# A gated recurrence with a highway layer: pairs of tokens, turned as 32-bit elements

## The chip, the cores and the metric

The kernel runs on one core of one Trainium2 chip. The metric is the device time of one execution in microseconds (us). Before the change three runs took 226.25, 229.24 and 226.26 us, a median of 226.26 us.

A core has five engines that matter here, each with its own instruction queue that it works through in order: TensorE (PE in the profile; its weight loads are listed apart, as PEld), VectorE (DVE), ScalarE (ACT), GpSimd (POOL), and SyncE (SP), which only issues transfers. Transfers between the chip's memory (HBM) and the on-chip memory (SBUF) run on 16 DMA engines. TensorE writes its results to a small memory of its own, PSUM, which VectorE and ScalarE can read.

## The reference, cut to what matters

```python
# x, f_logit: 4 sequences x 6336 tokens x 256 channels, float32
sig = 1.0 / (1.0 + np.exp(-f_logit))
f = lower_bound + (1.0 - lower_bound) * sig      # decay, per token and channel
i = 1.0 - f
for t in range(S):
    h = f[:, t] * h + i[:, t] * x[:, t]          # a scan along the tokens of each sequence
    y[:, t] = h

# then, over all 25344 tokens, with y in the place of x:
H = np.maximum(y @ w_h, 0.0)
T = 1.0 / (1.0 + np.exp(-(y @ w_t + b_t)))
out = T * H + (1.0 - T) * y
```

## The kernel before, in words

The 25,344 tokens are cut into units. Most units are 1024 consecutive tokens of one sequence; the two first units hold 192 tokens of each of two sequences, the first sequence's first 1024 tokens are cut into two units of 512, and the last 1024 into units of 512, 256 and 256. Units of different sequences alternate.

Tokens come from HBM with the tokens on the partitions: a tile `lt` (gate logits) and a tile `xt` (inputs) of 128 partitions x 8 token columns x 256 channels, float32. `load` (line 80) puts token `j*128 + p` of the unit into column `j` of partition `p`, so each piece that a transfer reads in HBM is one token's row, 256 x 4 bytes = 1 KB. The two first units use two transfers for each tile (line 84).

Per unit, these steps follow, each in a function of its own:

- `gate` (ACT, line 143): u = sigmoid(-f_logit) as 16-bit floats. Since i = (1 - lower_bound) * u, u is all that is needed of the gate.
- `product` (POOL, line 156): bv = u * x as bf16, in four instructions of two token columns each.
- `decay_pe` and `b_pe` (PE, lines 182 and 196): the recurrence runs along the tokens, and a scan runs along a partition. So u and bv are transposed on TensorE, 128 tokens x 128 channels at a time, into the PSUM tiles `uT` and `bT` with channels on the partitions and the unit's tokens in order along them. A transpose is a weight load of the 128 x 128 block followed by a matmul with an identity matrix. There are two channel halves (index `h` or `m`), so a full unit has 2 x 8 transposes of u and as many of bv.
- `decay_act` (ACT, line 189): f = 1 - (1 - lower_bound) * uT, for one channel half, out of PSUM.
- `scan` (DVE, line 207): h = f*h + bT, for one channel half, one instruction over the unit's tokens, bT read straight out of PSUM. The state here is y divided by (1 - lower_bound); the constant is put into the weights instead.
- `z_pe` and `g_pe` (PE, line 218): the two products with w_t and w_h, tiles `zp` and `gp`.
- `t_act` (ACT, line 231), `d_dve` and `e_dve` (DVE, lines 237 and 249, a quarter of e on POOL, line 251): the sigmoid, the maximum with the skip term subtracted, and their product.
- `o_pe` (PE, lines 267 and 268): y and e are turned back to tokens on partitions and summed in PSUM. `o_act` (ACT, line 276) copies them out and `store` writes them.

The main loop is a software pipeline written out by hand. In iteration n it issues the loads of unit n+4, the gate and product of n+2, the turning and decay of n+1, the scans of n, the two weight products and d, e of n-1, and the output of n-2. `pin` keeps the instructions of an engine in the order in which they are written, so each engine's queue is fixed. Every PSUM tile has one buffer: `bT` of one channel half can be written only when the scan of the half before has read it. `follow` makes the unit's first `product` instruction wait for the e of the same iteration on DVE.

On DVE an iteration is: scan of half 0, d of half 0, scan of half 1, d of half 1, e. On PE, `b_pe(n, 1)` stands between the two scans and before `z_pe(p, 1)`, and `b_pe(n + 1, 0)` is followed by `decay_pe(n + 1, 1)` and `g_pe(n, 0)`.

On SP the loads and stores stand in one queue. Loads run ahead of their use as far as five buffers for each of `lt` and `xt` allow. The transfers of all queues share eight completion counters, so that the ninth transfer waits for the first.

Of the kernel before, what the change touches and what calls it, by code (L numbers as in the profile page):

```python
# [11 lines left out]
FP32 = mybir.dt.float32  # L12
BF16 = mybir.dt.bfloat16
FP16 = mybir.dt.float16
AF = mybir.ActivationFunctionType
# [4 lines left out]
def kernel(  # L20
# [16 lines left out]
    nc = tc.nc  # L37
    B, S, D = x.shape
    assert D == 256
    P = 128  # L40
    NH = D // P
    NB = 8
# [5 lines left out]
    units = []  # L48
# [4 lines left out]
    for s0 in range(rest, S, NB * P):  # L53
        for b in range(B):
            last = s0 + NB * P == S and b == B - 1
            a = s0
# [5 lines left out]
    singles = ctx.enter_context(tc.tile_pool(name="singles", bufs=1))  # L62
    inp = ctx.enter_context(tc.tile_pool(name="inp", bufs=5))
    upool = ctx.enter_context(tc.tile_pool(name="upool", bufs=3))
    mid = ctx.enter_context(tc.tile_pool(name="mid", bufs=2))
# [5 lines left out]
    st = [dict() for _ in range(NU)]  # L71

    def pin(ins):
        return tc.keep_in_program_order(ins)

    def load(n, name, src):
        np_, nb, _, b, a = units[n]
        t = inp.tile([P, NB, D], FP32, tag=name, name=name)
        if isinstance(b, int):
            pin(nc.sync.dma_start(t[:, :nb], src[b, a:a + nb * P, :].rearrange("(j p) d -> p j d", p=P)))  # L80
        else:
            t4 = t[:np_, :nb].rearrange("p (b j) d -> p b j d", j=2)
            for j in range(2):
                pin(nc.sync.dma_start(t4[:, :, j], src[b, a + j * np_:a + (j + 1) * np_, :].rearrange("b p d -> p b d")))
        st[n][name] = t

    def store(n, j0, j1):
# [19 lines left out]
    for n in range(2):  # L107
        load(n, "lt", f_logit)
        load(n, "xt", x)

    ident_b = singles.tile([P, P], BF16, name="ident_b")
    make_identity(nc, ident_b)
    ident_h = singles.tile([P, P], FP16, name="ident_h")
    make_identity(nc, ident_h)

# [23 lines left out]

    def gate(n):  # L140
        np_, nb = units[n][:2]
        u = upool.tile([P, NB, D], FP16, tag="u")
        pin(nc.scalar.activation(u[:np_, :nb], st[n]["lt"][:np_, :nb], AF.Sigmoid, scale=-1.0))  # L143
        st[n]["u"] = u

    def follow(ins, after):

        if after is not None:
            tc.add_manual_dep(ins.ins, after.ins.name, mybir.DependencyInfo(
                mybir.DependencyClass.Sync, mybir.DependencyReason.DATA), reason="shared port")  # L150

    def product(n, after):
        np_, nb = units[n][:2]
        bv = mid.tile([P, NB, D], BF16, tag="bv")
        for q in range(0, nb, 2):
            ins = pin(nc.gpsimd.tensor_mul(bv[:np_, q:q + 2], st[n]["u"][:np_, q:q + 2], st[n]["xt"][:np_, q:q + 2]))  # L156
            if q == 0:
                follow(ins, after)
        st[n]["bv"] = bv

    def width(n):
        return units[n][0] * units[n][1]

    def both(n, m, key, make):


        if width(n) > 512:
            st[n][key, m] = make()
            yield st[n][key, m], m, 0
        elif m == 0:  # L170
            st[n][key, 0] = st[n][key, 1] = t = make()
            for k in range(NH):
                yield t, k, k * 512

    def col(n, m):
        return 0 if width(n) > 512 else m * 512

    def decay_pe(n, m):
        np_, nb = units[n][:2]
        for uT, h, c in both(n, m, "uT", lambda: ps1.tile([P, NB * P], FP16, tag="uT", name="uT")):  # L180
            for j in range(nb):
                pin(nc.tensor.transpose(uT[:, c + j * np_:c + (j + 1) * np_], st[n]["u"][:np_, j, h * P:(h + 1) * P],  # L182
                                        ident_h[:np_, :np_]))

    def decay_act(n, h):
        N, c = width(n), col(n, h)
# [3 lines left out]
                                 scale=ncc[:, h:h + 1], bias=1.0))  # L190

    def b_pe(n, m):
        np_, nb = units[n][:2]
        for bT, h, c in both(n, m, "bT", lambda: ps1.tile([P, NB * P], BF16, tag="bT", name="bT")):
            for j in range(nb):
                pin(nc.tensor.transpose(bT[:, c + j * np_:c + (j + 1) * np_], st[n]["bv"][:np_, j, h * P:(h + 1) * P],  # L196
                                        ident_b[:np_, :np_]))

    carry = {}

# [81 lines left out]
    for n in range(-3, NU + 2):  # L282
        if ok(n + 4) and n + 4 > 1:
            load(n + 4, "lt", f_logit)
            load(n + 4, "xt", x)
        p, pp = n - 1, n - 2
# [11 lines left out]
        if ok(n + 1):  # L298
            decay_pe(n + 1, 0)
            decay_act(n + 1, 0)  # L300
        if ok(p):
            d_dve(p, 0)
        if ok(n):
            b_pe(n, 1)
# [10 lines left out]
        if ok(n + 2):  # L315
            gate(n + 2)
# [5 lines left out]
        if ok(n + 1):  # L322
            b_pe(n + 1, 0)
            decay_pe(n + 1, 1)
            decay_act(n + 1, 1)
# [4 lines left out]
        if ok(n + 2):  # L330
            product(n + 2, after)
# [32 lines left out]
```

## Time and profile before

| | |
|---|---|
| runs | 226.25, 229.24, 226.26 us; median 226.26 |
| the profiled execution | 229.01 us; its span, from first to last instruction, 226.9 us |
| busy over the span | PE 195.0 us (86%), DVE 202.1 (89%), ACT 199.1 (88%), POOL 140.0 (62%) |
| data moved | 78.69 MB, 52.43 MB of it read; 60,262 packets, 53,584 of them under 2 KB |
| one 1024-token unit in the middle of the run | 7.92 us |

The page divides the span into 40 slices of 5.7 us and gives, for each, the busy share of each engine in tenths (9 is 90% or more), the clock that TensorE was granted in tenths, and the rate of the transfers. The table of groups gives for each line of the kernel and each engine the number of instructions, their busy time, the mean of one in ns, and the time that the engine sat idle before them with what ended it. A timeline lists instructions in order of time: start and duration in us, engine, line, output<-input, how many were merged. Matmuls overlap in the pipeline of TensorE and their ends are modelled, so the distance between starts says what one costs in a row of them, and the duration says when the result is there.

### The profile page before, as it was taken

Reading aid. Unit: us, or ns where it says so; the run is one execution under the profiler, and the core shown is the slowest. Engines: PE = TensorE matmul, PEld = TensorE weight load, DVE = VectorE, ACT = ScalarE, POOL = GpSimd, SP = SyncE. Lnnn points to the kernel's source line nnn. Section 1 sums busy time; section 2 is a strip of 40 time slices with the busy share of each in tenths; the row PEclk is TensorE's granted clock in tenths of the full one; section 3 lists DMA queues with packets and bytes.
Section 4 is the critical chain, followed back from the end, with each engine's and each line's share of the span. In section 5 each row is a group of like instructions: output and inputs, shape, how many; then the busy total and the mean of one; then the engine's idle time right before and its main releaser. Section 6 shows DMA issues by size and latency. Waiting matters only on the chain.

```text
span 226.9 us, 4999 instructions
## 1 busy us (share of the span) xinstructions
PE 195.0 (86%) x2008; PEld 136.9 (60%) x2008; DVE 202.1 (89%) x159; ACT 199.1 (88%) x198; POOL 140.0 (62%) x131
## 2 busy tenths in 40 slices
PE   0588495989999999999999999999999999998971
PEld 0356365656766666676666657666665766665661
DVE  1499657799999999999999999999999999999871
ACT  4459946799999999999999999999999999976873
POOL 2654870745966786696678669667866966764300
PEclk9999857899999999999999999999999999999998
DMA  6999999999999999999999999999999997542444
GB/s 179 307 386 386 383 390 390 390 390 387 399 385 385 399 394 389 384 397 382 382 391 395 388 390 402 395 384 403 396 387 397 396 349 276 202 185 95 185 185 185
DMA packets 60262, 78.69 MB, mean 347 GB/s; under 512 B 2384, under 2 KB 53584, under 8 KB 60240
## 3 DMA queue, kind: packets, MB, share of 16 engines
q1 hardware_dynamic: 59152, 77.86, 93.9%
q10 hardware_dynamic: 1088, 0.53, 0.9%
q8 instruction: 15, 0.25, 0.4%
q14 instruction: 7, 0.06, 0.1%
HBM read 52.43 MB, written 25.95 MB: 345 GB/s over the span
## 4 chain that ended last, share of the span: by engine, by line
DVE 52%; issue 23%; PE 13%; DMA 4%; ACT 3%; POOL 3%; DVEq 0%; SPq 0%; ACTq 0%; POOLq 0%
DVE y L207 25%; DVE d L237 19%; DVE e L249 8%; PE gp L218 4%; PE zp L218 3%; POOL bv L156 3%; DMA xt<-in_x_dram 2%; PE bT L196 2%; PE uT L182 2%; DMA lt<-in_f_logit_dram 1%; PE op L267 1%; PE op L268 1%; ACT o L276 1%; ACT u L143 1%; ACT t L231 1%
## 5 line engine op out<-in xcount | busy, mean ns | idle before, releaser
L156 POOL TENSOR_TENSOR bv<-u,xt 128x512 bf16<-128x512 f16 (+1 forms) x100 | 114.3, 1172 | 18.9 <-DMA xt<-in_x_dram 7.2
L207 DVE TENSOR_TENSOR_SCAN y<-f,y,bT 128x1024 bf16<-128x1024 f16 (+2 forms) x54 | 113.7, 2105 | 7.9 <-PE bT L196 7.6
L231 ACT ACTIVATE t<-zp,bt 128x1024 bf16<-128x1024 f32 (+3 forms) x58 | 56.9, 994 | 13.5 <-PE zp L218 13.5
L218 PEld LDWEIGHTS <-w_sb 128*128 128x128 f16 x408 | 39.7, 100 | 43.1 <-issue 10.0
L237 DVE SCALAR_TENSOR_TENSOR d<-y,ncc,gp 128x1024 bf16<-128x1024 bf16 (+3 forms) x58 | 63.8, 1101 | 1.0 <-PE gp L218 0.9
L189 ACT ACTIVATE f<-uT,ncc 128x1024 f16<-128x1024 f16 (+3 forms) x58 | 58.4, 1007 | 4.2 <-PE uT L182 4.2
L251 POOL TENSOR_TENSOR e<-d,t 128x512 bf16<-128x512 bf16 x22 | 25.5, 1159 | 56.3 <-PE gp L218 56.3
L218 PE MATMUL gp<-y,w_sb 128*128 128x512 bf16 (+2 forms) x204 | 53.3, 385 | 3.7 <-DVE d L237 1.3
L218 PE MATMUL zp<-y,w_sb 128*128 128x512 bf16 (+2 forms) x204 | 52.6, 382 | 0.1
L267 PE MATMUL op<-diag,y 128*128 128x128 f16 (+1 forms) x400 | 50.8, 221 | 2.2 <-ACT o L276 2.2
L276 ACT COPY o<-op 128x1024 f32<-128x1024 f32 (+2 forms) x51 | 50.9, 997 | 1.9 <-PE op L268 1.7
L143 ACT ACTIVATE u<-lt 128x2048 f16<-128x2048 f32 (+3 forms) x29 | 49.0, 1689 | 3.9 <-DMA lt<-in_f_logit_dram 3.9
L268 PE MATMUL op<-ident_b,e 128*128 128x128 bf16 (+1 forms) x400 | 50.8, 220 | 0.0
L268 PEld LDWEIGHTS <-e 128*128 128x128 bf16 (+1 forms) x400 | 44.9, 115 | 7.5 <-POOL bv L156 1.3
L267 PEld LDWEIGHTS <-y 128*128 128x128 bf16 (+1 forms) x400 | 45.0, 114 | 5.7 <-issue 0.3
L196 PE MATMUL bT<-ident_b,bv 128*128 128x128 bf16 (+1 forms) x400 | 32.8, 224 | 16.6 <-DVE y L207 8.3
L196 PEld LDWEIGHTS <-bv 128*128 128x128 bf16 (+1 forms) x400 | 26.9, 100 | 23.8 <-issue 15.2
L182 PE MATMUL uT<-ident_h,u 128*128 128x128 f16 (+1 forms) x400 | 32.4, 227 | 5.7 <-ACT u L143 5.7
L182 PEld LDWEIGHTS <-u 128*128 128x128 f16 (+1 forms) x400 | 26.1, 103 | 6.1 <-ACT u L143 5.7
L249 DVE TENSOR_TENSOR e<-d,t 128x1536 bf16<-128x1536 bf16 (+3 forms) x29 | 25.9, 892 | 3.6 <-ACT t L231 0.8
L207 DVE TENSOR_TENSOR_SCAN y<-f,bT 128x192 bf16<-128x192 f16 x8 | 3.9, 536 | 4.1 <-PE bT L196 4.1
L117 DVE TENSOR_SCALAR cc<-lb 128x2 f32<-128x2 f32 x1 | 0.2, 169 | 3.8 <-DMA lb<-in_lower_bound_dram 3.8
(16 smaller groups left out, 6.8 us busy)
## 6 DMA issues: line engine op xcount, KB each, us to landing
out_dram<-o SPq DMA_DIRECT2D x47, 512.0 KB, 7.2
lt<-in_f_logit_dram SPq DMA_DIRECT2D x22, 1024.0 KB, 9.4
xt<-in_x_dram SPq DMA_DIRECT2D x22, 1024.0 KB, 11.3
lt<-in_f_logit_dram SPq DMA_DIRECT2D x3, 512.0 KB, 7.6
xt<-in_x_dram SPq DMA_DIRECT2D x3, 512.0 KB, 6.7
lt<-in_f_logit_dram SPq DMA_DIRECT2D x4, 192.0 KB, 3.7
xt<-in_x_dram SPq DMA_DIRECT2D x4, 192.0 KB, 3.9
out_dram<-o SPq DMA_DIRECT2D x2, 384.0 KB, 9.3
```

Of the source, the lines that this page charges most:

```text
L143: pin(nc.scalar.activation(u[:np_, :nb], st[n]["lt"][:np_, :nb], AF.Sigmoid, scale=-1.0))
L156: ins = pin(nc.gpsimd.tensor_mul(bv[:np_, q:q + 2], st[n]["u"][:np_, q:q + 2], st[n]["xt"][:np_, q:q + 2]))
L182: pin(nc.tensor.transpose(uT[:, c + j * np_:c + (j + 1) * np_], st[n]["u"][:np_, j, h * P:(h + 1) * P], ident_h[:np_, :np_]))
L189: pin(nc.scalar.activation(st[n]["f"][:, h, :N], st[n]["uT", h][:, c:c + N], AF.Identity, scale=ncc[:, h:h + 1], bias=1.0))
L196: pin(nc.tensor.transpose(bT[:, c + j * np_:c + (j + 1) * np_], st[n]["bv"][:np_, j, h * P:(h + 1) * P], ident_b[:np_, :np_]))
L207: pin(nc.vector.tensor_tensor_scan(y[:, h, c0:c0 + ln], st[n]["f"][:, h, c0:c0 + ln], st[n]["bT", h][:, col(n, h) + c0:col(n, h) + c0 + ln ...
L218: pin(nc.tensor.matmul(p[:, c + a:c + e], w_sb[:, k, ki, h * P:(h + 1) * P], st[n]["y"][:, ki, a:e], start=ki == 0, stop=ki == NH - 1))
L231: pin(nc.scalar.activation(st[n]["t"][:, m, :N], st[n]["zp", m][:, c:c + N], AF.Sigmoid, bias=bt[:, m:m + 1]))
L237: pin(nc.vector.scalar_tensor_tensor(st[n]["d"][:, m, :N], st[n]["y"][:, m, :N], ncc[:, m:m + 1], st[n]["gp", m][:, c:c + N], op0=ALU.mult ...
L267: pin(nc.tensor.matmul(o, st[n]["y"][:, h, cols], diag[:, h], start=True, stop=False))
L268: pin(nc.tensor.matmul(o, st[n]["e"][:, h, cols], ident_b, start=False, stop=True))
L276: pin(nc.scalar.copy(st[n]["o"][:np_, j0:j1], st[n]["op"][:np_, :j1 - j0]))
```

## The change

Each partition now takes two neighbouring tokens, so that a load reads runs of two rows (2 KB): token `256k + 2p + j` goes to column `2k + j` of partition `p`. The two first units need one transfer for each tile instead of two.

The tiles `u` and `bv` keep the two 16-bit values of a channel side by side, in the order (token pair, channel, token of the pair). `gate` and `product` therefore write, and `product` reads, 16-bit elements with a step of two elements; their shapes and numbers stay.

The two 16-bit values together are taken as one float32 element for the transposes. `turn` transposes a 128 x 128 block of such elements, that is 256 tokens x 128 channels, against a float32 identity, into the same bytes of `uT` and `bT`: the 16-bit values land in token order, so decay, scan and all that follows read what they read before. A full unit has 2 x 4 such transposes of u and as many of bv. A third identity, `ident_f`, is made at the start.

```diff
+    def pairs(t):
+        return t.rearrange("p (k j) d -> p k (j d)", j=2)
+    def inner(t):
+        return t.rearrange("p k d j -> p k j d")
     def load(n, name, src):
...
-            pin(nc.sync.dma_start(t[:, :nb], src[b, a:a + nb * P, :].rearrange("(j p) d -> p j d", p=P)))
+            pin(nc.sync.dma_start(pairs(t[:, :nb]), src[b, a:a + nb * P, :].rearrange("(k p j) d -> p k (j d)", p=P, j=2)))
         else:
-            t4 = t[:np_, :nb].rearrange("p (b j) d -> p b j d", j=2)
-            for j in range(2):
-                pin(nc.sync.dma_start(t4[:, :, j], src[b, a + j * np_:a + (j + 1) * np_, :].rearrange("b p d -> p b d")))
+            pin(nc.sync.dma_start(pairs(t[:np_, :nb]), src[b, a:a + 2 * np_, :].rearrange("b (p j) d -> p b (j d)", j=2)))
...
+    ident_f = singles.tile([P, P], FP32, name="ident_f")
+    make_identity(nc, ident_f)
...
-        u = upool.tile([P, NB, D], FP16, tag="u")
-        pin(nc.scalar.activation(u[:np_, :nb], st[n]["lt"][:np_, :nb], AF.Sigmoid, scale=-1.0))
+        u = upool.tile([P, NB // 2, D, 2], FP16, tag="u")
+        pin(nc.scalar.activation(inner(u[:np_, :nb // 2]), st[n]["lt"][:np_, :nb].rearrange("p (k j) d -> p k j d", j=2),
+                                 AF.Sigmoid, scale=-1.0))
...
-        bv = mid.tile([P, NB, D], BF16, tag="bv")
-        for q in range(0, nb, 2):
-            ins = pin(nc.gpsimd.tensor_mul(bv[:np_, q:q + 2], st[n]["u"][:np_, q:q + 2], st[n]["xt"][:np_, q:q + 2]))
+        bv = mid.tile([P, NB // 2, D, 2], BF16, tag="bv")
+        for k in range(nb // 2):
+            ins = pin(nc.gpsimd.tensor_mul(inner(bv[:np_, k:k + 1])[:, 0], inner(st[n]["u"][:np_, k:k + 1])[:, 0],
+                                           st[n]["xt"][:np_, 2 * k:2 * k + 2]))
...
+    def turn(n, t, key, h, c):
+        np_, nb = units[n][:2]
+        for k in range(nb // 2):
+            pin(nc.tensor.transpose(t[:, c + 2 * k * np_:c + 2 * (k + 1) * np_].bitcast(FP32),
+                                    st[n][key][:np_, k, h * P:(h + 1) * P].rearrange("p d j -> p (d j)").bitcast(FP32),
+                                    ident_f[:np_, :np_]))
+
     def decay_pe(n, m):
...
-            for j in range(nb):
-                pin(nc.tensor.transpose(uT[:, c + j * np_:c + (j + 1) * np_], st[n]["u"][:np_, j, h * P:(h + 1) * P],
-                                        ident_h[:np_, :np_]))
+            turn(n, uT, "u", h, c)
...
     def b_pe(n, m):
...
-            for j in range(nb):
-                pin(nc.tensor.transpose(bT[:, c + j * np_:c + (j + 1) * np_], st[n]["bv"][:np_, j, h * P:(h + 1) * P],
-                                        ident_b[:np_, :np_]))
+            turn(n, bT, "bv", h, c)
```

In the built program each transpose is one weight load and one matmul, as before: 400 of each in the place of 800. On SP four transfers fall away, those of the two first units; on POOL two instructions come in at the start, for `ident_f`. The order of all engines is otherwise the same.

More of the change, by code (lines that the diff above doesn't have):

```diff
@@ L153, in product @@
         np_, nb = units[n][:2]
-        bv = mid.tile([P, NB, D], BF16, tag="bv")
-        for q in range(0, nb, 2):
-            ins = pin(nc.gpsimd.tensor_mul(bv[:np_, q:q + 2], st[n]["u"][:np_, q:q + 2], st[n]["xt"][:np_, q:q + 2]))
-            if q == 0:
+        bv = mid.tile([P, NB // 2, D, 2], BF16, tag="bv")
+        for k in range(nb // 2):
+            ins = pin(nc.gpsimd.tensor_mul(inner(bv[:np_, k:k + 1])[:, 0], inner(st[n]["u"][:np_, k:k + 1])[:, 0],
+                                           st[n]["xt"][:np_, 2 * k:2 * k + 2]))
+            if k == 0:
                 follow(ins, after)
@@ L176, in col @@
         return 0 if width(n) > 512 else m * 512
+    def turn(n, t, key, h, c):
[4 more added lines that the diff above has]
+                                    ident_f[:np_, :np_]))
     def decay_pe(n, m):
-        np_, nb = units[n][:2]
         for uT, h, c in both(n, m, "uT", lambda: ps1.tile([P, NB * P], FP16, tag="uT", name="uT")):
-            for j in range(nb):
-                pin(nc.tensor.transpose(uT[:, c + j * np_:c + (j + 1) * np_], st[n]["u"][:np_, j, h * P:(h + 1) * P],
-                                        ident_h[:np_, :np_]))
+            turn(n, uT, "u", h, c)
     def decay_act(n, h):
@@ L192, in b_pe @@
     def b_pe(n, m):
-        np_, nb = units[n][:2]
         for bT, h, c in both(n, m, "bT", lambda: ps1.tile([P, NB * P], BF16, tag="bT", name="bT")):
-            for j in range(nb):
-                pin(nc.tensor.transpose(bT[:, c + j * np_:c + (j + 1) * np_], st[n]["bv"][:np_, j, h * P:(h + 1) * P],
-                                        ident_b[:np_, :np_]))
+            turn(n, bT, "bv", h, c)
     carry = {}
```

## The prediction

> **What bounds the kernel now.** I read the slices of the page first, to see which engine is full and when.
>
> ```profile
> PE   0588495989999999999999999999999999998971
> DVE  1499657799999999999999999999999999999871
> ACT  4459946799999999999999999999999999976873
> PEclk9999857899999999999999999999999999999998
> GB/s 179 307 386 386 383 390 390 390 390 387 399 385 385 399 394 389 384 397 382 382 391 395 388 390 402 395 384 403 396 387 397 396 349 276 202 185 95 185 185 185
> ```
>
> After about 44 us three engines show 9 in every slice. The transfers stay at 385 to 400 GB/s and fall off from slice 32 (182 us), 40 us before the end: loads run ahead and are not awaited. The waits agree: ACT waited for `lt` three times (3.9 us) and POOL for `xt` three times (7.2 us), all before 14 us. So I asked for busy time in one period of the middle, 7.92 us (columns: PE, PEld, DVE, ACT, POOL, clock, DMA share, GB/s).
>
> ```profile
> 107.30:115.22 7.92, 7.50 (x81) 5.28 (x80) 7.82 (x6) 7.75 (x8) 5.67 (x6) 1.00 1.07 390
> ```
>
> DVE is busy for 7.82 us of 7.92, ACT for 7.75, POOL for 5.67. PE's 7.50 is modelled; distances of starts are safer. The timeline shows what stands between two scans:
>
> ```profile
> 105.56 0.61 PE L182 MATMUL uT<-ident_h,u 128*128 128x128 f16 x8
> 106.13 1.26 DVE L237 SCALAR_TENSOR_TENSOR d<-y,ncc,gp 128x1024 bf16<-128x1024 bf16 x1
> 106.26 0.61 PE L196 MATMUL bT<-ident_b,bv 128*128 128x128 bf16 x8
> 106.70 1.03 PE L218 MATMUL zp<-y,w_sb 128*128 128x512 bf16 x4
> 107.30 2.34 DVE L207 TENSOR_TENSOR_SCAN y<-f,y,bT 128x1024 bf16<-128x1024 f16 x1
> ```
>
> Eight transposes start over 0.44 us (106.26 to 106.70), 55 ns each, and their results are there at 106.87, 0.43 us before the scan at 107.30 can start behind d. Four matmuls of 512 columns start over 0.87 us (106.70 to 107.57). PE's demand per period is then 16 x 0.217 + 32 output matmuls x 0.055 + 32 transposes x 0.055 = 3.47 + 1.76 + 1.76 = 7.0 us of 7.92. DVE sets the period; PE has 0.9 us to spare, ACT 0.17, POOL 2.25.
>
> ```profile
> L156 POOL TENSOR_TENSOR bv<-u,xt 128x512 bf16<-128x512 f16 (+1 forms) x100 | 114.3, 1172 | 18.9 <-DMA xt<-in_x_dram 7.2
> L143 ACT ACTIVATE u<-lt 128x2048 f16<-128x2048 f32 (+3 forms) x29 | 49.0, 1689 | 3.9 <-DMA lt<-in_f_logit_dram 3.9
> L182 PE MATMUL uT<-ident_h,u 128*128 128x128 f16 (+1 forms) x400 | 32.4, 227 | 5.7 <-ACT u L143 5.7
> ```
>
> **What the Trainium skill says.** "TensorE: Matmul & The Clock Gate", Terms: weight loads and matmuls have a transpose mode that is "4× faster for FP32". No float32 transpose is in this trace, so nothing here confirms it. The same page, Weight-path perf modes: the fast weight load, on for 128 weights, is not used for FP32 input; LDWEIGHTS (loading the stationary operand) gives columns / 1.2 ns, 107 ns for 128. In the trace 16-bit loads last 98 ns but follow each other every 55 ns, so they overlap; float32 is not shown. "GPSIMD Engine Reference", Performance pitfalls: reads cost about half as much again once step x element size passes 8 bytes; here it becomes 4, and the trace has no stepped row. "SBUF — State Buffer", Door 1: up to 8 bf16 of step are free within a 16-byte line; the step here is two.
>
> **The change, part by part.** Call the cost of one float32 transpose in a row of them t.
>
> Transposes: removed are 32 x 0.055 = 1.76 us of PE per period, added 16 t. The low end of t is 55 ns, as for 16 bits (a gain of 0.88 us per period on PE, worth at most the 0.1 us of DVE idleness, 2 us in all); the high end is 4 x 55 = 222 ns, four passes. I take 110 ns, the skill's unhurried weight load with the matmul beside it: 16 x 0.110 = 1.76 us, nothing gained, nothing lost. Also, the first weight load of each group was done ahead of the wait for the scan (it ended at 106.05 for a matmul at 106.26); in the new program the wait stands before the weight load, so each of the groups behind a scan starts some 0.1 us later (estimate from the 98 ns). The cover is d: from the scan's end at 106.21, 0.06 + 0.10 + 4 x 0.110 + 0.17 to the last result gives 106.98, against 107.30. The other group, bT and uT in a row, must end before the d that frees `gp` at 102.89: 101.71 + 0.16 + 8 x 0.110 = 102.75. Both hold, so the period stays at 7.92 us. Without that cover each late 0.1 us would cost 20.6 x 0.1 = 2 us, since (207 - 44) / 7.92 = 20.6 periods run at DVE's pace. Behind the waiting transposes stand zp and gp, for which t (ACT) and d (DVE) wait.
>
> From which t does PE decide? 3.47 + 1.76 + 16 t + 0.2 (two late starts) = 7.92 at t = 156 ns.
>
> Gate: 22 full instructions of 1927 ns, same element count, output in steps of two. I take the same duration. Low end: nothing in the row could get shorter. High end, if each 16-bit write took twice its slot: +1.8 us per period, 1.6 us beyond ACT's spare time, +34 us. Product: four instructions at 1.14 us per period. I take the same; they could not be quicker than the equal-sized contiguous e on POOL (1159 ns); high end +50%: bv would end 2.3 us later. At 109.76 it ends now, and the scan that needs it starts at 111.79, about 0.3 us of transposing in between: 1.7 us of slack for the scan, less for PE behind it. Decides from about +25%.
>
> Loads: the same bytes in half as many packets. In the middle nobody waits for them, so a quicker transfer is worth nothing: the five buffers are the cover. At the start the rate is only 261 to 295 GB/s between 2 and 10 us, as the two `xt` transfers of unit 1 wait for counters of earlier ones; with four transfers fewer they need not, and `xt` of unit 1, which lands at 9.7 us on the chain that ended last, may come 2 us sooner. But w_sb, behind weights that land at about 10.8 us, is finished by DVE at 13.2 us, and the first gp starts at 12.8. So 2 us at most, 0 at least; I take 0.4. `ident_f` ends on POOL by some 2.4 us, while the first product waits until 5.90: free.
>
> Sum for the profiled execution: 229.0 + 0 - 0.4 = 228.6 us. It was 2.75 us above the median of the three runs, so against the median: 226.26 - 0.4, about 226.
>
> **The rivals.**
> *PE becomes the bound (slower).* At t = 222 ns PE needs 3.47 + 1.76 + 3.55 + 0.2 = 8.98 us per period, 1.06 more than DVE: 20.6 x 1.06 = 22, plus about 1 at the ends, 249 us. It decides from t = 156 ns. For it: half the number of instructions does not mean half the work, the float32 load is not the fast one, and PE is already at 88% of the period by starts. Against it: the transpose mode of the skill. In between, if load (107) and matmul (55) don't overlap, t is 162 ns and the period 8.02: +2 to +4 us; at 180 ns 8.31, +8: 229 to 235, and 240 at 200 ns.
> *A stepped access slows POOL or ACT.* Product +40% makes bv end 1.8 us late per period, about 0.7 beyond what scan and PE absorb: 20.6 x 0.7 = 14, 240 us. For it: ACT has just 0.17 us to spare. Against: steps of 4 bytes lie below both limits named above.
> *The start becomes quicker (faster).* PE's clock falls to half between 26.6 and 34 us (the 8, 5, 7 in its row), after PE waited for bv, and DVE idles 1.58 + 3.45 + 1.35 us around it, waiting for bT. If the earlier loads shift this and the half clock is missed, up to 6 us go: 220. Against: the work before it is bound by ACT and POOL one after the other, not by loads.
> That the transposes are still split into passes on the chip would be the first rival.
>
> **How the numbers follow.** Forecast, DVE keeps its pace: 0.42, 223 to 230 us. PE as bound at about 249: 0.20; PE in between, 231 to 240: 0.16; a stepped access, about 240: 0.14; quicker start, about 220: 0.08. A measurement of this kernel tells 2%, 4.5 us, from no change: below 221.7, up to 230.8, above. So faster 0.08, same 0.42, slower 0.50. The forecast is the single likeliest case; the range has to reach into the slower ones: leaving out the faster case and the part of the first rival above 250 (some 0.10) gives 222 to 250.
>
> **What would show it.** Right: DVE still busy 7.8 us in a period of 7.92, transposes with 110 ns between starts, gate and product rows within 3% of 1927 and 1171 ns, the packets under 2 KB mostly gone. Wrong: scans that wait for bT in the middle of the run, ACT waiting for zp more than the present 13.5 us, transposes over 156 ns apart; or POOL over 1.4 us per product; or PEclk below 9 in the middle.

## The result: 237.3 us, slower by about 4%

The changed kernel took 237.48, 234.91, 237.53 and 237.07 us, a median of 237.27, against 226.33 for the kernel before (226.25 to 229.24 in four runs): a ratio of 1.043, with a 95% interval of 1.032 to 1.053. Executions take longer at a lower mean clock of TensorE (the kernel before: medians of 226.6 us at 0.988 to 0.991 and 229.1 at 0.973 to 0.974, over its later executions), and of the changed kernel's four three had 0.974 and one 0.983; at equal clock it is 7 to 8.5 us slower, 3.2 to 3.7%. The execution profiled is the one of 237.48 us, with a span of 235.7 us. The one of before took 229.01 us with a span of 226.9, so 8.8 us of span are to be explained between two profiles in which TensorE had the same mean clock, 0.974.

The slices, first the changed kernel's:

```profile
PE   0459758789999999999999999999999999998972
DVE  1289763979999999999999999999999999999872
ACT  4527985699999999999999999999999999997883
PEclk9999976799999999999999999999999999999998
DMA packets 34851, 78.64 MB, mean 334 GB/s; under 512 B 2320, under 2 KB 2832, under 8 KB 34832
```

Three engines still show 9 throughout the middle, TensorE's clock too, and the packets under 2 KB went from 53,584 to 2,832, so the loads do what the change says. Tenths can't tell which of the three engines is full. The chain of work that ended last can. Its shares by engine, in the kernel before:

```profile
DVE 52%; issue 23%; PE 13%; DMA 4%; ACT 3%; POOL 3%; DVEq 0%; SPq 0%; ACTq 0%; POOLq 0%
```

and in the changed one:

```profile
ACT 53%; PE 16%; DVE 12%; issue 9%; DMA 5%; POOL 2%; ACTq 0%; DVEq 0%; POOLq 0%
```

DVE has lost the chain and ACT has it: 3% became 53%. The busy times in the changed kernel's middle say the same (columns: PE, PEld, DVE, ACT, POOL, clock, DMA share, GB/s):

```profile
107.30:115.22 7.92, 7.40 (x63) 4.94 (x61) 7.65 (x6) 7.92 (x8) 5.84 (x6) 1.00 1.03 366
120.00:140.00 20.00, 18.95 (x162) 12.91 (x160) 19.25 (x13) 20.00 (x20) 15.83 (x14) 1.00 1.03 397
```

In the first window, which the prediction shows for the kernel before, ACT is now busy for all of the 7.92 us (before 7.75) and DVE for 7.65 (before 7.82). In the second, ACT is busy for all of 20.00 us; before it was 19.50, and DVE 19.79. Where the time came in is read from the starts of the 1024-token scans on DVE, two for each unit:

| | before | after | difference |
|---|---|---|---|
| start of the fourth 1024-token scan | 43.90 us | 48.91 us | +5.0: the start |
| from there to the start of the last one | 158.46 | 162.30 | +3.8: the middle |
| from there to the end of the span | 24.5 | 24.5 | 0 |

**The middle.** A period is the distance from one unit's scan to the same scan of the next unit. After the fourth 1024-token scan, four periods took 7.92 us, one 8.04, fourteen 8.19 and the last 7.93. The timeline of ACT shows what grew; before:

```profile
98.91 1.13 ACT L189 ACTIVATE f<-uT,ncc 128x1024 f16<-128x1024 f16 x1
99.92 1.12 ACT L231 ACTIVATE t<-zp,bt 128x1024 bf16<-128x1024 f32 x1
100.92 1.93 ACT L143 ACTIVATE u<-lt 128x2048 f16<-128x2048 f32 x1
102.72 1.03 ACT L276 COPY o<-op 128x1024 f32<-128x1024 f32 x1
103.61 1.15 ACT L189 ACTIVATE f<-uT,ncc 128x1024 f16<-128x1024 f16 x1
104.92 1.11 ACT L231 ACTIVATE t<-zp,bt 128x1024 bf16<-128x1024 f32 x1 [0.16 <-PE zp L218]
```

and after, a whole unit:

```profile
107.33 2.74 ACT L151 ACTIVATE u<-lt 128x2048 f16<-128x2048 f32 x1
109.70 1.23 ACT L288 COPY o<-op 128x1024 f32<-128x1024 f32 x1
110.59 1.36 ACT L204 ACTIVATE f<-uT,ncc 128x1024 f16<-128x1024 f16 x1
111.59 1.36 ACT L243 ACTIVATE t<-zp,bt 128x1024 bf16<-128x1024 f32 x1
112.59 1.27 ACT L288 COPY o<-op 128x1024 f32<-128x1024 f32 x1
113.48 1.39 ACT L204 ACTIVATE f<-uT,ncc 128x1024 f16<-128x1024 f16 x1
114.49 1.39 ACT L243 ACTIVATE t<-zp,bt 128x1024 bf16<-128x1024 f32 x1
115.48 2.79 ACT L151 ACTIVATE u<-lt 128x2048 f16<-128x2048 f32 x1
```

Every duration is longer than before, which misleads: instructions of ACT overlap (o starts at 109.70, while the gate ends at 107.33 + 2.74 = 110.07). The distances between starts say what each costs the queue. For o, f and t they are as before, 0.89, 1.0 and 1.0 us (the last pair of the lines from before, 103.61 to 104.92, holds a wait for `zp`). For the gate it was 102.72 - 100.92 = 1.80 us and is 109.70 - 107.33 = 2.37 us: +0.57 us, or 0.28 ns for each of 2048 elements. By distances ACT needed 1.80 + 2 x (0.89 + 1.01 + 1.00) = 7.60 us per unit before, 0.32 less than DVE; now it needs 8.17.

**The start.** The first sigmoid t (ACT, L243) comes at 18.46 us, where it came at 15.63. Followed back on the changed kernel's chain, it stood behind this:

```profile
5.16 7.78 DMA w_raw<-in_moe_w_h_dram
...
13.91 1.41 DVE w_sb L142
15.35 1.24 DVE w_sb L144
17.14 1.28 PE zp L230 x4
```

The transfer of the weight w_h is issued on ACT's queue at 5.16 us and lands at 12.94; before, it was issued at 5.00 and took 5.8. DVE then scales the weights into `w_sb`, by 16.6 us in the place of 13.2. Of this, 2.2 us are the later begin (13.03 in the place of 10.80); the other 1.1 us are that two of the four instructions took 1.49 and 1.23 us by the timeline, while a product ran on POOL (13.72 to 16.43), where before only one was as long, 1.12 us. That the product slows them was not tested.

**Transposes and product**, which the prediction cared most about; the changed kernel's timeline of PE, and its group of the product:

```profile
103.82 0.66 PE L192 MATMUL uT<-ident_f,u 128*128 128x128 f32 x4
104.31 0.60 PE L192 MATMUL bT<-ident_f,bv 128*128 128x128 f32 x4
104.82 1.02 PE L230 MATMUL zp<-y,w_sb 128*128 128x512 bf16 x4
```

```profile
L165 POOL TENSOR_TENSOR bv<-u,xt 128x512 bf16<-128x512 f16 (+1 forms) x100 | 125.4, 1289 | 21.5 <-DMA xt<-in_x_dram 6.5
```

Four float32 transposes start over 0.49 to 0.51 us, 0.12 to 0.13 each. The product went from 1171 to 1289 ns, +10%.

### The profile page after: what moved, and what is told of

It is laid out like the page before. It is cut to its first block, busy times and chain, and to the rows that moved or that the text cites. A ratio compares the mean times of both kernels' runs of the same rounds, so it can differ in the third digit from the quotient of the medians.

```text
span 235.7 us, 4221 instructions
## 1 busy us (share of the span) xinstructions
PE 200.1 (85%) x1608; PEld 135.0 (57%) x1608; DVE 205.0 (87%) x159; ACT 210.6 (89%) x198; POOL 151.5 (64%) x133
## 2 busy tenths in 40 slices
DMA packets 34851, 78.64 MB, mean 334 GB/s; under 512 B 2320, under 2 KB 2832, under 8 KB 34832
## 4 chain that ended last, share of the span: by engine, by line
ACT 53%; PE 16%; DVE 12%; issue 9%; DMA 5%; POOL 2%; ACTq 0%; DVEq 0%; POOLq 0%
ACT u L151 18%; ACT o L288 15%; ACT t L243 12%; ACT f L204 8%; DVE y L219 6%; PE gp L230 4%; PE zp L230 4%; DMA w_raw<-in_moe_w_h_dram 3%; DVE d L249 3%; PE uT L192 3%; POOL bv L165 2%; PE op L279 2%; PE bT L192 2%; PE op L280 2%; DMA lt<-in_f_logit_dram 2%
## 5 line engine op out<-in xcount | busy, mean ns | idle before, releaser
L165 POOL TENSOR_TENSOR bv<-u,xt 128x512 bf16<-128x512 f16 (+1 forms) x100 | 125.4, 1289 | 21.5 <-DMA xt<-in_x_dram 6.5
L219 DVE TENSOR_TENSOR_SCAN y<-f,y,bT 128x1024 bf16<-128x1024 f16 (+2 forms) x54 | 113.7, 2106 | 12.1 <-PE bT L192 10.3
L243 ACT ACTIVATE t<-zp,bt 128x1024 bf16<-128x1024 f32 (+3 forms) x58 | 69.3, 1208 | 12.2 <-PE zp L230 12.2
L204 ACT ACTIVATE f<-uT,ncc 128x1024 f16<-128x1024 f16 (+3 forms) x58 | 70.7, 1219 | 4.0 <-PE uT L192 4.0
L151 ACT ACTIVATE u<-lt 128x2048 f16<-128x2048 f32 (+3 forms) x29 | 70.2, 2420 | 2.9 <-DMA lt<-in_f_logit_dram 2.9
L230 PEld LDWEIGHTS <-w_sb 128*128 128x128 f16 x408 | 40.8, 100 | 46.8 <-issue 8.8
L288 ACT COPY o<-op 128x1024 f32<-128x1024 f32 (+2 forms) x51 | 63.2, 1238 | 1.8 <-PE op L280 1.8
L192 PE MATMUL bT<-ident_f,bv 128*128 128x128 f32 (+1 forms) x200 | 34.4, 291 | 11.6 <-DVE y L219 6.5
L192 PE MATMUL uT<-ident_f,u 128*128 128x128 f32 (+1 forms) x200 | 33.2, 291 | 7.0 <-ACT u L151 6.2
L192 PEld LDWEIGHTS bT<-ident_f,bv 128*128 128x128 f32 (+1 forms) x200 | 23.2, 147 | 17.0 <-POOL bv L165 7.4
L192 PEld LDWEIGHTS uT<-ident_f,u 128*128 128x128 f32 (+1 forms) x200 | 23.7, 149 | 9.7 <-issue 6.4
```

What stands on the lines that cost most here:

```text
L151: pin(nc.scalar.activation(inner(u[:np_, :nb // 2]), st[n]["lt"][:np_, :nb].rearrange("p (k j) d -> p k j d", j=2), AF.Sigmoid, scale=-1.0))
L165: ins = pin(nc.gpsimd.tensor_mul(inner(bv[:np_, k:k + 1])[:, 0], inner(st[n]["u"][:np_, k:k + 1])[:, 0], st[n]["xt"][:np_, 2 * k:2 * k + 2]))
L192: pin(nc.tensor.transpose(t[:, c + 2 * k * np_:c + 2 * (k + 1) * np_].bitcast(FP32), st[n][key][:np_, k, h * P:(h + 1) * P].rearrange("p d ...
L204: pin(nc.scalar.activation(st[n]["f"][:, h, :N], st[n]["uT", h][:, c:c + N], AF.Identity, scale=ncc[:, h:h + 1], bias=1.0))
L219: pin(nc.vector.tensor_tensor_scan(y[:, h, c0:c0 + ln], st[n]["f"][:, h, c0:c0 + ln], st[n]["bT", h][:, col(n, h) + c0:col(n, h) + c0 + ln ...
L230: pin(nc.tensor.matmul(p[:, c + a:c + e], w_sb[:, k, ki, h * P:(h + 1) * P], st[n]["y"][:, ki, a:e], start=ki == 0, stop=ki == NH - 1))
```

## The experiments

The theory after the result: the step of two 16-bit elements makes the gate 0.57 us longer, ACT takes the pace from DVE, and that is the whole of the middle; the late weights, together with the longer gate, are the start. The rival: scans now wait 14.6 us for `bT` from PE (19 waits, most of them 0.17 us in the middle), so the float32 transposes hold the scans, and ACT is only full of waiting. All ratios below are against the kernel before, run on the same chip (medians 226.4 to 227.3 us); they are not the quotients of two medians.

**The gate writes in one run.** Only the output's order changes.

```diff
-        pin(nc.scalar.activation(inner(u[:np_, :nb // 2]), st[n]["lt"][:np_, :nb].rearrange("p (k j) d -> p k j d", j=2),
-                                 AF.Sigmoid, scale=-1.0))
+        pin(nc.scalar.activation(u[:np_, :nb // 2].rearrange("p k d j -> p (k d j)"),
+                                 st[n]["lt"][:np_, :nb].rearrange("p j d -> p (j d)"), AF.Sigmoid, scale=-1.0))
```

> The changed kernel with the gate writing its output in one run again: the two values of a channel are then not side by side, so u goes to wrong places; every other instruction is as in the changed kernel. Theory of two causes: the gate falls from 2.37 to 1.80 us from its start to the next one's, ACT has slack again, the middle returns from 8.19 to 7.92 us per unit (3.8 us) and the start gains about 1 us: 232 to 233.5 us. Rival (float32 transposes hold up the scans, which wait for bT 14.6 us in all): the scans still wait, 236 to 238 us.

Measured: 229.84 us, ratio 1.012 (0.997 to 1.028), lower than expected. All periods are 7.92 us, the gate is back at 1.80 us, and ACT has idle time again:

```profile
120.00:140.00 20.00, 19.10 (x168) 13.15 (x168) 19.79 (x13) 19.61 (x19) 16.37 (x15) 1.00 1.04 403
```

The float32 transposes and the stepped product are still in this kernel, so neither holds the middle. Scans wait for `bT` only four times here, none of them in the middle. The rival falls: the 0.17 us for which scans wait in the changed kernel are a consequence, since PE waits for ACT there (17 times for o, 9.7 us). The next experiment shows the same: its transposes are the 16-bit ones, and scans wait for `bT` 19 times as well (12.1 us).

**The same ACT time, put into the kernel before.**

```diff
         st[n]["u"] = u
+        if nb == NB:
+            more = mid.tile([P, 576], FP16, tag="more")
+            pin(nc.scalar.activation(more, st[n]["lt"].rearrange("p j d -> p (j d)")[:, :576], AF.Sigmoid, scale=-1.0))
```

> The kernel before with one more ScalarE instruction in each full unit, a sigmoid of 576 elements into a tile that nobody reads, some 0.57 us from its start to the next one's, as much as the step costs in the changed gate; results are unchanged. If ACT's pace explains the middle of the changed kernel: 8.15 to 8.22 us per unit after some units at 7.92, 231 to 233 us. If the stepped gate does harm by something else than its time on ACT: 7.92 us and 226 to 228 us.

Measured: 232.79 us, ratio 1.021 (1.015 to 1.028). Four periods of 7.92 us, then one of 8.00, then 8.22; from the fourth 1024-token scan to the last 162.69 us (before 158.46, after 162.30). The timeline of ACT in this kernel:

```profile
140.69 2.46 ACT L143 ACTIVATE u<-lt 128x2048 f16<-128x2048 f32 x1
142.49 1.24 ACT L146 ACTIVATE more<-lt 128x576 f16<-128x576 f32 x1
143.06 1.57 ACT L279 COPY o<-op 128x1024 f32<-128x1024 f32 x1
```

The added instruction takes 0.57 us of the queue, and with nothing else of the change in place, the middle of the changed kernel appears. Note the gate: the old one, 1.80 us to the next start, but its duration is 2.46 us, where it was 1.93 with ACT not full. The changed kernel's longer durations of f, t and o are of this kind.

**Can the step be moved to the read side?** The gate reads the two tokens alternately and writes in one run; the values land where they belong.

```diff
-        pin(nc.scalar.activation(inner(u[:np_, :nb // 2]), st[n]["lt"][:np_, :nb].rearrange("p (k j) d -> p k j d", j=2),
+        pin(nc.scalar.activation(u[:np_, :nb // 2], st[n]["lt"][:np_, :nb].rearrange("p (k j) d -> p k d j", j=2),
```

> The changed kernel with the step moved to the other side of the gate: it reads lt alternating between the two rows of a pair (256 float32 elements apart) and writes u in one run; what is computed is the same. If the step in the output is what costs: the gate is back at 1.80 us and the time at 232 to 233.5 us. If any broken run costs ACT, or the read costs more because each element lies on another line: the gate is at 2.4 us or above, 237 us or more.

Measured: 234.77 us, ratio 1.037 (1.024 to 1.049), between the two expectations, and on ACT:

```profile
144.79 2.88 ACT L151 ACTIVATE u<-lt 128x2048 f16<-128x2048 f32 x1
147.06 1.51 ACT L288 COPY o<-op 128x1024 f32<-128x1024 f32 x1
```

2.27 us, +0.47: that only writing with a step costs is wrong. The periods are 8.10 us. This gives three doses of one rule, period = the larger of 7.92 and 7.60 plus what was added: 8.07, 8.17 and 8.17 us expected, 8.10 (this kernel), 8.19 (the changed one) and 8.22 (the added instruction) measured. Why the first periods still take 7.92 us was not tested. That ACT is some 1.2 us ahead then, and loses 0.27 us per period in the changed kernel (four periods and a longer one) and 0.18 here (six and a longer one), fits; it is an estimate from these periods.

**At which price would the transposes decide?** With the gate in one run, each transpose of u is done twice.

```diff
         for uT, h, c in both(n, m, "uT", lambda: ps1.tile([P, NB * P], FP16, tag="uT", name="uT")):
+            turn(n, uT, "u", h, c)
             turn(n, uT, "u", h, c)
```

> The kernel of the experiment with the gate in one run, with each float32 transpose of u done twice (24 per full unit instead of 16); u is in wrong places as there. The balance of PE (3.47 + 1.76 + 24 x 0.118 + 0.2 = 8.26 us against 7.92 for DVE) says that PE just becomes the bound: 8.2 to 8.4 us per unit, about 7 us more than with 16, 235 to 238 us. If PE had more room than the starts show: 7.92 us and about 230 us.

Measured: 234.51 us in two executions, ratio 1.030 (1.021 to 1.038), periods of 8.03 to 8.09 us, less than expected; PE is busy for 19.84 us of the stretch from 120 to 140 us. The timeline of PE:

```profile
142.93 1.04 PE L192 MATMUL uT<-ident_f,u 128*128 128x128 f32 x8
143.81 0.60 PE L192 MATMUL bT<-ident_f,bv 128*128 128x128 f32 x4
```

Eight start over 0.88 us, 0.110 each; the expectation had reckoned with 0.118. The prediction's balance for PE, with 24 in the place of 16, is 3.47 + 1.76 + 24 x 0.110 + 0.2 = 8.07 us: it holds to 0.04 us. So with 16 the transposes leave PE at 7.19 us, 0.7 short of DVE (7.40 with the 0.123 of a group of four).

**The loads alone, on the kernel before.** Only `load` is changed, as in the changed kernel.

```diff
-            pin(nc.sync.dma_start(t[:, :nb], src[b, a:a + nb * P, :].rearrange("(j p) d -> p j d", p=P)))
+            pin(nc.sync.dma_start(pairs(t[:, :nb]), src[b, a:a + nb * P, :].rearrange("(k p j) d -> p k (j d)", p=P, j=2)))
...
-            t4 = t[:np_, :nb].rearrange("p (b j) d -> p b j d", j=2)
-            for j in range(2):
-                pin(nc.sync.dma_start(t4[:, :, j], src[b, a + j * np_:a + (j + 1) * np_, :].rearrange("b p d -> p b d")))
+            pin(nc.sync.dma_start(pairs(t[:np_, :nb]), src[b, a:a + 2 * np_, :].rearrange("b (p j) d -> p b (j d)", j=2)))
```

> The kernel before with the new loads alone (runs of two rows, four transfers fewer at the start); the tokens of a pair then stand in another order, so what is computed belongs to reordered tokens, and every instruction keeps its shape. Theory of two causes (late weights at the start, stepped gate in the middle): the queue of loads is fuller when the weights are fetched, w_raw lands near 12.9 us instead of 10.8, the first zp starts 2 to 3 us later, the middle stays at 7.92 us per unit: 228 to 230 us. Rival (the start is late because the new gate, product and transposes are slower, not because of the loads): 225 to 227 us, as before or a little under.

Measured: 228.66 us, ratio 1.009 (1.005 to 1.014), with periods of 7.92 us. The first t comes at 17.95 us (before 15.63), and DVE waited for the weight:

```profile
12.67 0.49 DVE L136 TENSOR_SCALAR w_sb<-w_raw,cc 128x512 f16<-128x512 f32 x1 [1.03 <-DMA w_raw<-in_moe_w_h_dram]
```

So the new loads alone, longer runs and four transfers fewer together, delay the start, and no part of the gate is needed for that.

**The changed kernel with the old loads.** The reverse of that diff; all else stays changed.

```diff
-            pin(nc.sync.dma_start(pairs(t[:, :nb]), src[b, a:a + nb * P, :].rearrange("(k p j) d -> p k (j d)", p=P, j=2)))
+            pin(nc.sync.dma_start(t[:, :nb], src[b, a:a + nb * P, :].rearrange("(j p) d -> p j d", p=P)))
...
```

> The changed kernel with the loads of before (one row per run, eight transfers for the two first units): the pairs are then pairs of tokens 128 apart, so the scan runs over reordered tokens; shapes and numbers of all other instructions stay. Theory of two causes: weights land near 10.8 us, the first zp starts 2 to 3 us earlier, the middle stays at 8.19 us: 233.5 to 235 us. Rival (start late because of slower gate, product and transposes): 236.5 to 238 us.

Measured: 232.37 us, ratio 1.029 (1.011 to 1.046), a little less than expected. The first t is at 15.04 us, `w_sb` begins at 11.24 us; the periods stay at 8.19. Loads and gate are two separate causes.

**The weights ahead.** In the changed kernel, the weights and the bias go on SP behind the loads of units 0 and 1, before all later loads.

```diff
-            pin(nc.scalar.dma_start(w_raw[:, 1 - k], w.rearrange("(h p) o -> p h o", p=P)))
-        pin(nc.scalar.dma_start(bt, moe_b_t.rearrange("(h p) -> p h", p=P)))
+            pin(nc.sync.dma_start(w_raw[:, 1 - k], w.rearrange("(h p) o -> p h o", p=P)))
+        pin(nc.sync.dma_start(bt, moe_b_t.rearrange("(h p) -> p h", p=P)))
...
     for n in range(2):
         load(n, "lt", f_logit)
         load(n, "xt", x)
+    load_weights()
```

> The changed kernel with the three transfers of the weights moved to the SP queue, behind the loads of the two first units and ahead of all others. Theory of two causes: w_raw no longer shares the engines with later loads, lands by 9 us, the first t starts near 15.5 us instead of 18.5, and the whole comes 2.5 to 4 us earlier; the middle stays at 8.19 us per unit: 233 to 235 us. Rival (the start is bound by gate, product and transposes): within 1 us of the changed kernel, 236 to 238 us.

Measured: 232.25 us, ratio 1.021 (1.015 to 1.027), a little less than expected. The first t comes at 15.57 us with the new loads in place, the periods stay at 8.19: the lateness of the first t is gone, nothing of the loss in the middle.

The same edit in the kernel before (`load_weights` and the place of its call, nothing else):

```diff
-            pin(nc.scalar.dma_start(w_raw[:, 1 - k], w.rearrange("(h p) o -> p h o", p=P)))
+            pin(nc.sync.dma_start(w_raw[:, 1 - k], w.rearrange("(h p) o -> p h o", p=P)))
...
```

> The kernel before with the weights on the SP queue behind the loads of the two first units. In it the weights and the second unit's bv are ready within 1 us of each other, so earlier weights alone gain 0 to 1 us: 225.5 to 227.5 us, middle 7.92. If the weights alone held the start: 2 to 3 us less, 224 to 225 us.

Measured: 226.36 us, ratio 1.000 (0.997 to 1.003). The ratio shows no gain. At equal clock this kernel is 0.8 and 0.9 us faster (medians of 225.8 against 226.6 us at 0.988 to 0.991, 228.1 against 229.1 at 0.973 to 0.974), which lies within the expectation and is too little for the interval to show. No version that was run is clearly faster than the kernel before.

**Both causes taken out**: in the changed kernel, the gate in one run and the weights ahead.

```diff
-        pin(nc.scalar.activation(inner(u[:np_, :nb // 2]), st[n]["lt"][:np_, :nb].rearrange("p (k j) d -> p k j d", j=2),
+        pin(nc.scalar.activation(u[:np_, :nb // 2].rearrange("p k d j -> p (k d j)"),
...
-            pin(nc.scalar.dma_start(w_raw[:, 1 - k], w.rearrange("(h p) o -> p h o", p=P)))
+            pin(nc.sync.dma_start(w_raw[:, 1 - k], w.rearrange("(h p) o -> p h o", p=P)))
...
```

> The changed kernel with both suspected causes taken out at once: the gate writes its 2048 values in one run (so the values of u lie in other places and the output is not the reference's; the amount of every step's work is kept), and the two weights and the bias go on SP behind the loads of units 0 and 1. Theory (the gate's step costs the middle 3.8 us, the late weights cost the start up to 5 us, and nothing else of the change costs anything): first t at about 15.6 us, all periods 7.92 us, 226 to 228 us where the kernel before gives 226 to 227, ratio 0.995 to 1.01. Rival (the float32 transposes or the stepped product have a price of their own that the gate's hid): periods stay above 7.95 us or the ratio stays above 1.015, 230 us or more.

Measured: 227.31 us, ratio 1.006 (1.002 to 1.010), all periods 7.92 us, the first t at 15.64 us:

```profile
120.00:140.00 20.00, 18.96 (x159) 12.92 (x162) 19.79 (x13) 19.66 (x18) 16.13 (x14) 1.00 1.03 400
```

The two causes account for nearly all of the loss. The 0.6% that is left by the ratio goes with the clock: at 0.988 to 0.992 the median here is 226.7 us (kernel before 226.6), at 0.973 to 0.974 it is 229.3 (229.1). Against the kernel before with the weights ahead too, 225.8 and 228.1 us, some 1 us remains. It lies outside the middle and was not taken apart; the 10% of the product is a candidate that was only argued.

## Why the prediction was wrong

The forecast of no change, 226.0 us at a chance of 0.42, is refuted: slower, which had 0.50. The range of 222 to 250 holds the measured time by luck: its upper part came from TensorE as the bound, which did not happen, and from a stepped access at about 240 us that was priced on POOL.

- **The step that failed: "Gate: ... I take the same duration."** It measured +0.57 us in each full unit, a third of the high end that was priced (+1.8 us). The prediction had the number that makes this matter, ACT's spare time, at 0.17 us; it is 0.32 by the distances of starts. The sum is 0.57 - 0.32 = 0.25 us per unit; for fourteen periods 3.5 us, with the longer one before them 3.6, and 3.84 was measured. The error was to put the step at nothing, with no stepped row in any trace to price it. "SBUF — State Buffer", Door 1 (steps of up to 8 bf16 are free) was used for an engine that it doesn't name; on ACT the measurement contradicts it. "ScalarE: Activation LUTs", Rules for kernel authors, gives about 0.3 us plus 0.83 ns an element, an estimate of 2.0 us for 2048: the old gate's duration of 1.93 us is near it, and the rule has no term for a step. A bound had been worked out, and a price from 0.32 us on decides; with both ends open the step deserved more than the 0.14 it got, and on ACT: the rival "A stepped access slows POOL or ACT" named the right mechanism and worked out its price on the wrong engine.
- **Loads at the start: "2 us at most, 0 at least; I take 0.4."** The sign was wrong. The prediction saw that `w_sb` stood "behind weights that land at about 10.8 us" and held that fixed, while it moved the transfers beside them. With four transfers fewer, SP issues the loads of units 0 and 1 by 2.6 us (before: 4.8), and the next two at 4.91 and 5.36 us (before 5.75 and 6.83), so they stand beside the weights' transfers, and the weight w_h takes 7.78 us in the place of 5.8. "DMA: Bandwidth & Descriptors", Queues, rings and completion order, says that each engine takes turns between queues, a packet at a time; that fits, but whether the fuller queue or the doubled run takes the weights' share was not separated. The experiment with the weights ahead shows that this lateness is the cause: it brings the first t from 18.46 to 15.57 us.
- **How the start adds up.** In the changed kernel's profile the scans from 16.50 us on (before 13.17) are 2.9 to 3.3 us late; the new loads alone made the first t 2.3 us late. Then two scans wait 0.55 and 1.00 us for ACT's f, with the longer gates ahead of it, and the lateness grows to 3.6, 4.3 and in the end 5.0 us. As whole executions at a clock of 0.973 to 0.974, the changed kernel with both causes taken out took 229.3 us, with the late weights alone (gate in one run) 231.7, with the stepped gate alone (weights ahead) 234.2, and with both, as it is, 237.5. So the late weights cost 2.4 to 3.3 us and the gate 4.9 to 5.8, of which 3.8 in the middle. The two middle figures are single executions, and those of the kernel before spread over 1.4 us at this clock, so whether the two causes make each other worse is not settled.
- **Right: a float32 transpose costs 110 ns** in a row (0.110 to 0.128 us measured), and so is PE's balance, which the doubled transposes confirm to 0.04 us. The number was taken from the weight load's price in "TensorE: Matmul & The Clock Gate", 107 ns; here a float32 weight load lasts 140 ns in the middle, so the number is right and the reason for it not shown. The groups behind a scan start 0.14 us after its end (105.02 + 2.35 = 107.37, then 107.51), in the place of 0.05: the 0.1 us later that was reckoned with. PE as the bound, given 0.36 in all, didn't happen.
- **Right: the product is harmless.** It grew by 10%, below the 25% from which it would decide.
- **Right: in the middle nobody waits for loads,** so the packets saved bring nothing there. `ident_f` shows on no chain.
- **The signs listed.** "Scans that wait for bT in the middle of the run" came true and would have led to PE: it says that the forecast is wrong, but not why. The gate's row (1927 to 2782 ns) overstates, since ACT's durations are longer when it is full: in the experiment with the added instruction the old gate lasts 2.46 us at an unchanged distance of 1.80.
- **The quicker start did not come.** The prediction read one stretch of half clock, 26.6 to 34 us; by windows of 0.5 us the kernel before has two, 27 to 34 and 37.5 to 41 us. The changed kernel's profile has both as well, some 5 us later, 32.5 to 39 and 42.5 to 45.5 us.

## What to carry to other kernels

Before a layout change moves a step onto an engine, take each engine's spare time per period from the distances of its starts, and ask which unknown price exceeds it: with 0.3 us to spare of 7.9, a third more per element on one instruction is enough to change the bound. When an instruction is made cheaper for one engine by a layout, look at who now writes that layout. An earlier transfer can delay those beside it, as here the weights', which landed after 7.8 us in the place of 5.8: list all that are in flight then, and who waits for each.

## What the runs showed that was not expected

- On ACT a sigmoid of 128 x 2048 with 16-bit output takes 1.80 us of its queue in one run, 2.37 with an output step of two elements (4 bytes), and 2.27 when it reads float32 alternately from two rows 1 KB apart.
- On a full ACT the profile's durations are a fifth to a half longer (f 1.15 us before, 1.39 in the changed kernel and 1.72 with the added instruction), with unchanged distances.
- A product on POOL with output and one input in steps of two 16-bit elements: 1289 in the place of 1171 ns.
- In the middle a float32 weight load for a transpose lasts 140 ns (median), a 16-bit one 97 to 98, yet float32 transposes follow each other every 110 to 128 ns.
- The kernels in which both causes are present, the changed one and the one that reads with a step, had a clock of 0.974 to 0.983 in all eight executions; the kernel before had 0.988 or more in 42 of 63. Why was not followed up.
